# Two-bank PSUM copies, an earlier output 1, and weight-gradient units held for the end, in the backward pass of a grouped-query decode block

## The chip, the cores and the metric

The kernel runs on one core of one Trainium2 chip. The metric is the device time of one execution in microseconds (us), the median of several executions. The kernel before takes 1144.1 us (median of 4 runs, 1141.7 to 1148.9; the first three had a median of 1144.4).

The trace names the engines PE (TensorE matmul), PEld (its weight loads), DVE (VectorE), ACT (ScalarE), POOL (GpSimd, which issues the stores) and SP (SyncE, which issues the loads). Line numbers such as L1162 are lines of the kernel that was run, so the same statement has another number in each kernel; the text says which is which.

## The reference

Two layers, each an attention over a long key/value cache followed by an MLP, and then the gradients of everything with respect to a given output gradient. The sizes that matter: batch 2, one query position, 32 query heads over 4 key/value heads, 16384 cached positions, head size 128, model width 1024, MLP width 3584.

```python
x = A_x
x = x + A(layernorm(x), k_cache, v_cache, wq, wo)     # attention
x = x + B(layernorm(x), w1, b1, w2, b2)               # layernorm, gelu MLP
x = x + A(layernorm(x), ...);  x = x + B(layernorm(x), ...)
out, vjp = jax.vjp(f, A_x, k_cache, v_cache, wq, wo, w1, b1, w2, b2)
return out, *vjp(grad_out)    # out_0; dx = out_1; dK = out_2; dV = out_3; dwq = out_4; dwo, dw1, db1, dw2, db2
```

The outputs dK and dV are as large as the caches: 64 tiles of 1 MB, computed and stored in the last third of the kernel, together with about 32 MB of weight gradients. The caches are read several times in bf16. All of it passes through one core's DMA: 449 MB.

## The kernel before

The change touches the last third: the loop that works off chunks of the caches. In each step of that loop TensorE transposes V tiles, computes scores, and makes "pairs" (half a tile of dK or dV each) and "dW units" (512 columns of a weight gradient). Pairs and dW units are matmuls into PSUM, followed by copies that turn fp32 in PSUM into bf16 in SBUF. The Trainium skill ("PSUM — Partial Sum Buffer", Terms) says that PSUM has 8 banks of 2 KiB per partition and that one matmul's output fits in one bank, which is 512 fp32 columns; the matmuls of this loop agree, the widest writes 512 columns. Four banks go round for this work and for a few small products between (`X`); the other four serve transposes (2), an accumulator and small things.

```python
X = [px([128, 512], F32, "xm%d" % i) for i in range(4)]      # four tiles of one bank, in rotation
def mx(): return nxt("x", X)

def kv_pair(w, i, h):                                        # half a dK or dV tile
    ...
    pss = [mx() for _ in range(4)]
    for b in range(2):
        for r in range(4):
            PE.matmul(pss[r][:, b * 256:(b + 1) * 256], lhsT=blk[32 * r:32 * r + 32, ...], rhs=Qm[32 * r:32 * r + 32, ...], ...)
    for r in range(4):
        evac_cast(sv_[:, 2 * h:2 * h + 2, r], pss[r][:]..., 512)      # to ScalarE or VectorE, the less loaded
    if h == 1: store(...)                                    # 1 MB, issued by GpSimd

def dw_units(...):  # for each 512 columns:
        ps = mx()
        PE.matmul(ps[:], lhsT=xrows[p:p + 4, ...], rhs=yrows[p:p + 4, ...], ...)   # 4 rows
        evac_cast(sv_[:, j, c0:c0 + 512], ps[:], 512)
        # after the last of a tile: store(...)

def load_tile(): return (by_store or by_read).popleft()      # a tile whose store was issued, else one that was read

while 2 * m < NS + 12 or late or fill or late_pe or m <= max(v_at) + 2:
    ...                                                      # transposes, scores, pairs of this step
    step_fill(1 if m < NCH else 5)                           # 5 dW units of 512 columns
    pump(NLD + 3 if m < NCH else NLD, 3)                     # loads, at most 7 open
    m += 1
g0 = attn_in_bwd(0, g1, dn0)                                 # last layer-norm backward, after everything
col_to_row_f32(g0, DJ, out_1..., "o1")                       # output 1
```

A matmul into a bank waits until the copy out of it is done. The traces show matmuls starting in program order, so that what comes later in TensorE's queue waits too (an example with 1.04 us stands below, with the profile after).

## Time and profile before

| | before |
|---|---|
| median time | 1144.1 us |
| bytes moved | 449.3 MB, 394 GB/s over the span |
| middle, 840 to 1100 us | 422 GB/s, DMA full |
| opening of the last third, 730 to 840 us | 347 GB/s |
| from the last dqT (1115.95 us) to the end | 24.8 us at 220 GB/s |

The first lines are from the page of the kernel before: its span, TensorE's busy time, and the clock granted to TensorE (tenths) and the DMA rate in 40 equal slices of 28.5 us.

```profile
span 1140.8 us, 39972 instructions
PE 954.6 (84%) x17567; PEld 736.6 (65%) x17567; DVE 633.4 (56%) x1347; ACT 566.2 (50%) x1418; POOL 64.7 (6%) x117
...
PEclk9989785597999876999998899989779868896785
...
GB/s 371 424 424 424 425 423 413 408 379 354 423 424 424 425 302 424 410 377 407 373 423 419 349 354 355 314 331 309 400 423 422 421 420 422 423 422 421 424 419 247
```

Nine slices of the last third are at 420 GB/s or above and one at 419; the last slice is at 247. Windows give the same by stage. The columns: stretch, its length, then for each engine its busy us in the stretch and the number of instructions; then the granted clock, the DMA engines' mean busy share, and GB/s. The last two stretches are cut at the last dqT, the query gradient that the end of the kernel depends on.

```profile
840.00:900.00 60.00, 52.90 (x690) 32.89 (x687) 48.41 (x85) 46.09 (x89) 9.51 (x16) 0.86 1.02 422
900.00:1000.00 100.00, 91.55 (x1122) 55.10 (x1120) 77.11 (x135) 71.85 (x139) 16.33 (x28) 0.79 1.02 422
1000.00:1100.00 100.00, 90.25 (x1230) 56.22 (x1228) 76.76 (x135) 71.01 (x137) 14.25 (x24) 0.81 1.02 422
1100.00:1116.00 16.00, 11.69 (x129) 5.39 (x125) 11.67 (x20) 10.90 (x21) 2.14 (x4) 0.66 1.00 420
1116.00:1140.80 24.80, 14.57 (x114) 6.44 (x114) 10.63 (x26) 7.90 (x14) 3.15 (x5) 0.50 0.54 220
```

DMA is full until 1116 us. And beside it TensorE is busy 90 to 92 us of every 100, VectorE 77, ScalarE 71: the compute engines keep up with DMA, but not by much.

The stores of the tail, in order of time on GpSimd (start, duration, and in brackets how long GpSimd had been idle and for what):

```profile
1124.41 0.53 POOL L1126 DMA_DIRECT2D out_dram<-keepV  x1 [12.02 <-DVE keepV L166]
1126.29 0.53 POOL L1126 DMA_DIRECT2D out_dram<-keepK  x1 [1.35 <-ACT big L163]
1128.13 0.77 POOL L1126 DMA_DIRECT2D out_dram<-big  x1 [1.31 <-ACT big L163]
1131.17 0.77 POOL L1126 DMA_DIRECT2D out_dram<-big  x1 [2.27 <-ACT big L163]
1136.65 0.55 POOL L202 DMA_DIRECT2D out_dram<-o_row  x1 [4.71 <-DVE o_row L201]
```

No store is issued for 12 us, and output 1 is the last.

### The profile page before, as it was taken

The page shows a single profiled execution, that of the slowest core. Times are in us where ns is not written, and L with a number is a line of the kernel's source. Part 1 is how long each engine was busy: PE and PEld are TensorE (multiplying, and loading weights), DVE is VectorE, ACT ScalarE, POOL GpSimd, SP SyncE. Part 2 cuts the span into 40 slices and gives each one's busy share as a digit, 9 for nine tenths or more (in the row PEclk, how much of TensorE's full clock was granted, in tenths as well). Part 3 has the DMA queues.
Part 4 walks back from the last instruction along what each step waited for, and adds up shares of the span by engine and source line. Part 5 has one row for each costly group of instructions (what it writes and reads, how often), then busy time and mean ns, then how long its engine had stood idle before and what let it go on. Part 6 is the DMA issues. An engine that isn't in the chain of part 4 may idle for free. (4 is left out here: it accounts for less than half of the span.)

```text
span 1140.8 us, 39972 instructions
## 1 busy us (share of the span) xinstructions
PE 954.6 (84%) x17567; PEld 736.6 (65%) x17567; DVE 633.4 (56%) x1347; ACT 566.2 (50%) x1418; POOL 64.7 (6%) x117
## 2 busy tenths in 40 slices
PE   4988896487879885899987789988898989999885
PEld 3867674387767765888776688765555555555552
DVE  1535442133545433544845355768678868786784
ACT  0534351022535330344554444668677767776673
POOL 0000000000000000000000000001111112111111
PEclk9989785597999876999998899989779868896785
DMA  9999999998999989999999999887999999999996
GB/s 371 424 424 424 425 423 413 408 379 354 423 424 424 425 302 424 410 377 407 373 423 419 349 354 355 314 331 309 400 423 422 421 420 422 423 422 421 424 419 247
DMA packets 89130, 449.30 MB, mean 394 GB/s; under 512 B 7026, under 2 KB 7026, under 8 KB 49788
## 3 DMA queue, kind: packets, MB, share of 16 engines
q1 hardware_dynamic: 72204, 348.17, 75.4%
q0 software_dynamic: 16752, 98.59, 20.8%
q8 instruction: 137, 2.24, 0.7%
q14 instruction: 37, 0.30, 0.1%
HBM read 348.14 MB, written 98.58 MB: 392 GB/s over the span
## 5 line engine op out<-in xcount | busy, mean ns | idle before, releaser
L155 ACT COPY kT<-tp 128x512 int32<-128x512 int32 x209 | 122.8, 587 | 252.0 <-PE tp L421 243.3
L158 DVE COPY kT<-tp 128x1024 bf16<-128x1024 bf16 x159 | 108.6, 691 | 109.2 <-PE tp L421 97.3
L421 PE MATMUL tp<-ident,kv_K 128*128 128x128 bf16 x1728 | 144.5, 233 | 4.5 <-DMA kv_K<-in_A_k_cache_dram 4.4
L421 PEld LDWEIGHTS <-kv_K 128*128 128x128 bf16 x1728 | 109.6, 104 | 5.3 <-DMA kv_K<-in_A_k_cache_dram 5.2
L166 DVE CAST big<-xm 128x512 bf16<-128x512 f32 x135 | 88.1, 686 | 25.3 <-PE xm L1162 11.7
L163 ACT CAST big<-xm 128x512 bf16<-128x512 f32 x162 | 88.3, 594 | 24.6 <-PE xm L1162 12.7
L574 PEld LDWEIGHTS <-kT 128*128 128x128 bf16 x2048 | 76.6, 98 | 27.8 <-issue 21.4
L574 PE MATMUL sc<-qT_bf,kT 128*128 128x8 bf16 x2048 | 92.0, 171 | 0.3 <-issue 0.3
L538 ACT ACTIVATE e_all<-sc,negm 128x64 bf16<-128x64 f32 x256 | 77.1, 345 | 1.1 <-DVE negm L533 1.0
L307 PEld LDWEIGHTS <-wt 128*128 128x128 bf16 x1696 | 49.2, 104 | 43.7 <-issue 14.8
L421 PE MATMUL tp<-ident,kv_V 128*128 128x128 bf16 x864 | 70.1, 227 | 8.5 <-DMA kv_V<-in_A_v_cache_dram 7.6
L271 PE MATMUL wtp<-ident,wt 128*128 128x128 bf16 x928 | 73.9, 225 | 3.7 <-issue 2.5
L166 DVE CAST keepK<-xm 128x512 bf16<-128x512 f32 x91 | 59.1, 686 | 21.7 <-PE xm L1244 17.7
L453 PE MATMUL acc_all<-kv_V,e_all 128*16 128x256 bf16 x864 | 46.5, 296 | 26.4 <-DMA kv_V<-in_A_v_cache_dram 13.7
L163 ACT CAST keepK<-xm 128x512 bf16<-128x512 f32 x105 | 56.8, 594 | 23.8 <-PE xm L1244 23.1
L158 DVE COPY wT<-wtp 128x1024 bf16<-128x1024 bf16 (+1 forms) x64 | 40.7, 641 | 46.6 <-PE wtp L271 43.5
L155 ACT COPY wT<-wtp 128x512 int32<-128x512 int32 (+1 forms) x60 | 34.3, 572 | 61.7 <-PE wtp L271 47.5
L421 PEld LDWEIGHTS <-kv_V 128*128 128x128 bf16 x864 | 55.4, 102 | 10.7 <-DMA kv_V<-in_A_v_cache_dram 8.3
L166 DVE CAST keepV<-xm 128x512 bf16<-128x512 f32 (+1 forms) x80 | 52.5, 686 | 16.3 <-PE xm L1244 12.8
L163 ACT CAST keepV<-xm 128x512 bf16<-128x512 f32 (+1 forms) x93 | 50.3, 593 | 20.1 <-PE xm L1244 18.2
L538 ACT ACTIVATION_READ_ACCUMULATOR e_all<-sc,negm 128x1 f32 x256 | 60.1, 235 | 0.0
L271 PEld LDWEIGHTS <-wt 128*128 128x128 bf16 x928 | 56.3, 100 | 4.4 <-issue 3.0
(350 smaller groups left out, 1786.9 us busy)
## 6 DMA issues: line engine op xcount, KB each, us to landing
kv_K<-in_A_k_cache_dram SPq DMA_DIRECT2D x81, 1024.0 KB, 12.3
kv_V<-in_A_v_cache_dram SPq DMA_DIRECT2D x81, 1024.0 KB, 12.1
out_dram<-big POOLq DMA_DIRECT2D x36, 1024.0 KB, 18.5
wt<-in_A_wo_dram SPq DMA_DIRECT2D x32, 1024.0 KB, 10.2
wt<-in_B_w_dram SPq DMA_DIRECT2D x32, 896.0 KB, 14.2
out_dram<-keepK POOLq DMA_DIRECT2D x21, 1024.0 KB, 18.3
out_dram<-keepV POOLq DMA_DIRECT2D x19, 1024.0 KB, 15.0
wt<-in_A_wq_dram SPq DMA_DIRECT2D x16, 1024.0 KB, 9.0
```

The source lines that it names most:

```text
L155: S.copy(out=dst.bitcast(I32), in_=src.bitcast(I32))
L158: V.tensor_copy(out=dst, in_=src)
L163: S.copy(out=dst, in_=src)
L166: V.tensor_copy(out=dst, in_=src)
L271: PE.transpose(tp[:, o, :], wv[:, j, (o0 + o) * 128:(o0 + o + 1) * 128], ident[:])
L307: PE.matmul(fps[:, jo, :].rearrange("p (a b) -> p a b", b=2), lhsT=wv[:, j, jo * 128:(jo + 1) * 128], rhs=xT_bf[:, j0 + j, :].unsqueeze(1) ...
L421: PE.transpose(tp[:, j, :], cv[:, b * 8 + j, :], ident[:])
L453: PE.matmul(self.acc[cg:cg + 16, :], lhsT=coef(u), rhs=self.cv[:, t:t + 2, :].rearrange("p t d -> p (t d)"), start=False, stop=True, tile_ ...
L538: S.activation(out=e_all[:, g, f * half:(f + 1) * half, l, h, :], in_=sc[g][f][:, h, :].rearrange("p (a b) -> p a b", b=2), func=ACT.Exp, ...
L574: PE.matmul(sc[g][f][:, :, t % TH], lhsT=kT[:, j, :], rhs=q_bf[:, g, :], start=True, stop=True)
```

## The change

Its intent: fewer, larger copies out of PSUM; an opening that prefetches more; stores left over for the end so that DMA has work while the last query gradient is finished; and output 1 not at the very end.

```diff
 # 1. two-bank copies (in pairs and in dW units)
-    X = [px([128, 512], F32, "xm%d" % i) for i in range(4)]
+    XX = [ps_xx.tile([128, 2, 512], F32, name="xx%d" % i, tag="xx") for i in range(2)]
+    X = [XX[i // 2][:, i % 2, :] for i in range(4)]            # single banks are halves of these
-        for r in range(4):
-            evac_cast(sv_[:, 2 * h:2 * h + 2, r], pss[r][:]..., 512)
+        for r in range(2):
+            evac_cast(sv_[:, 2 * h:2 * h + 2, 2 * r:2 * r + 2]..., pss[r][:]..., 1024)
-                for c0 in range(0, ny, 512): ...                # dW: one matmul, one copy of 512
+                for c0 in range(0, ny, 1024): ...               # dW: two matmuls, one copy of 1024
 # 2. opening
-        return (by_store or by_read).popleft()
+        return (by_read or by_store if opening["on"] else by_store or by_read).popleft()
-    pump(NLD + 3, 4)
+    pump(NLD + 3, 3)
     ... two weight loads two chunks later; score banks swapped; two zero copies gone
 # 3. dW units held for the last ten steps, fewer loads open there
-        step_fill(1 if m < NCH else 5)
-        pump(NLD + 3 if m < NCH else NLD, 3)
+        step_fill(1 if m < NCH else 3 if m >= MF else 2 + bool(late), 0 if m >= MF else 20)
+        pump(NLD + 3 if m < NCH else NLD if m < MF + 4 else NLD - 1, 3)
 # 4. last dq to output 1 at once (and the last chunk's accumulation one step earlier)
+            tail.extend(in_rows(quarters[kv], kv))              # products, layer-norm backward, output 1
-    g0 = attn_in_bwd(0, g1, dn0)                                # was after the loop
-    col_to_row_f32(g0, DJ, out_1..., "o1")
 # 5. last dWq over 128 partitions, padded with zeros, stored in three pieces
     ... (cut: columns padded so that the transposes for dW rows write 32 rows)
+            late.extend(dw_units(nz, qz, None, [(0, 4), (4, 2), (6, 2)], 0, D, ...))
```

The bytes that move stay the same.

## The prediction

> **What bounds the kernel now.** The 16 DMA engines: the slice rows show them 98 to 102 % busy at 421 to 424 GB/s in most of the span, and 449.3 MB at 424 GB/s would take 1060 us (an estimate) of the 1140.8. The Trainium skill ("DMA: Bandwidth & Descriptors", Measured) gives 425 GB/s for a large transfer; the trace agrees. Only stretches in which DMA starves can pay. By the windows, 800 to 1116 us runs at 410 to 423 GB/s: nothing to win. Before 700 us the change touches almost nothing. Two stretches are left:
>
> - The tail. In 4 us windows from 1116 us: 256, 35, 272, 398, 388, 13 GB/s. Those 24.8 us move about 5.5 MB, 13 us of work at 424: some 12 us are lost. The chain that ended last shows why: last dqT at 1115.95, dq transposed and copied until 1118.1, dWq matmuls and pairs until 1131.2, no store issued from 1111.9 to 1124.4; then the last layer-norm backward (1130.5 to 1132.8), fp32 transposes and a 0.68 us cast twice, and the output-1 store at 1136.65.
> - The opening, 730 to 790 us: 306, 229, 367, 351, 243, 279 GB/s in 10 us windows, about 18 us lost. The SP queue's waits there are loads held by the landing of an older store from their tile (52 us in 4 waits), while ScalarE and VectorE are 76 to 96 % busy from 750 to 790.
>
> **What the change does.**
> 1. Two-bank copies: two 128x512 copies take 1.29 us on VectorE and 1.07 on ScalarE; one of 1024 about 1.22 and 1.05 (an estimate from 0.686 and 0.594 single). 0 to 2 us, all in the opening. Back-to-back pairs now wait for a whole two-bank copy, so their 1.8 us period does not shrink.
> 2. Opening: loads go first to tiles freed by compute, one more tile may be taken, two weight loads come two chunks later, two 0.6 us zero copies vanish. I give this 5 us of the 18; the copy engines limit the rest.
> 3. dW held: the instruction order shows 4 MB more dW stores among the last ones. The last loads run ahead of them, so the last dq comes earlier and stores are queued while dq is finished. This fills most of the hole around 1120.
> 4. Output 1 at once: its chain runs between the last pairs; the 5 us between the last big store's issue and output 1's leave the end.
> 5. Zero-padded dWq: the tail's clock is 0.50 although PE is 70 to 88 % busy with 4-row operands; 128 rows may raise it, 16 matmuls from 0.43 to about 0.22 us, hardly 1 us in effect since copies then bind.
>
> Tail: 12 us lost become about 4 (output 1 ended 4 us after its issue), so 8. Sum: 8 + 5: 1144.4 - 13 = **1131 us**, range 1122 to 1141. Chances: faster by over 2 % 0.09, within 2 % 0.90, slower 0.01.
>
> **What would show it.** Bytes stay 449 MB. Right: windows of the last 25 us near 400 GB/s without the 35 GB/s hole, the last dqT several us earlier, output 1's store no longer last by 5 us; shorter waits of loads on store landings in 730 to 790; the middle still at 421 to 424. Step 5: clock above 0.5 at the end.
>
> **What would make it wrong.** The held dW copies load ScalarE and VectorE (already 88 to 92 % busy at 1093 to 1103), the last steps become copy-bound and dq does not come earlier; the opening keeps its gap or moves it later because tiles are merely taken sooner; the coarser PSUM hand-over starves the copies; or the opening recovers all 18 us, over 2 %.

## More of the kernel before

How TensorE and the copies hand PSUM over shows in the waits of the middle, 840 to 1100 us (columns: who waited for whom, us in all, times, longest). L1162 is the dW matmul, L166 and L163 are the copies on VectorE and ScalarE.

```profile
PE xm L1162 <- ACT big L163: 2.5, 7, 0.5
...
PE xm L1162 <- DVE big L166: 2.1, 7, 0.6
```

All such waits of the dW matmul add up to 8 us there.

## The result, and the profile after

The changed kernel is correct and takes 1195.3 us (median of 4 runs, 1192.9 to 1197.1). Ratios in this document are the mean time of one kernel's runs over that of the kernel before in the same rounds, so they are not quite the ratio of the medians quoted. Here the ratio is 1.044, with a 95% interval of 1.040 to 1.048: slower by 4.4%, where 1131 us had been forecast, and slower given a chance of 1%.

The same lines of the page after (slices of 29.8 us):

```profile
span 1193.1 us, 39480 instructions
PE 974.3 (82%) x17567; PEld 749.6 (63%) x17567; DVE 622.2 (52%) x1174; ACT 559.6 (47%) x1225; POOL 68.1 (6%) x120
...
PEclk9988895588989957999988999977778677676675
...
GB/s 374 424 424 425 424 425 412 406 304 423 424 425 424 413 338 415 369 395 373 422 419 344 372 347 350 329 350 377 371 369 397 394 369 406 350 362 349 345 214 212
```

The copies did become cheaper: VectorE and ScalarE are busy 11 and 7 us less, in 366 fewer instructions. But from slice 30 on the DMA rate stays below 400 in every slice but one, where it was 419 or more until the last. The windows of the kernel after, cut at its last dqT (1165.3 us):

```profile
840.00:900.00 60.00, 50.93 (x617) 31.37 (x614) 40.69 (x47) 39.04 (x51) 7.64 (x13) 0.74 0.98 390
900.00:1000.00 100.00, 82.81 (x1034) 50.71 (x1033) 65.91 (x78) 62.61 (x81) 13.43 (x23) 0.76 0.99 392
1000.00:1100.00 100.00, 85.33 (x961) 51.23 (x959) 61.44 (x73) 59.30 (x74) 15.99 (x24) 0.69 0.92 356
1100.00:1165.30 65.30, 53.79 (x588) 32.56 (x584) 40.81 (x47) 38.77 (x47) 8.13 (x14) 0.71 0.70 287
1165.30:1193.10 27.80, 15.88 (x130) 6.57 (x130) 12.34 (x23) 9.01 (x9) 4.14 (x7) 0.56 0.51 209
```

Call "lost" the length of a stretch times (1 - rate / 424), the time in which DMA could have moved what it did not. Before: 1.2 us lost from 840 to 1100, 0.2 from there to the last dqT, 11.9 in the tail. After: 28.4, 21.1 and 14.1. The difference is 50.3 us, and the spans differ by 52.3. So nearly the whole loss is in the middle and its continuation, in the stretch of which the prediction had said "nothing to win", and where there was much to lose. All engines do less per microsecond there, TensorE too. Nobody is busier: somebody waits. The page says the same in its chain of work that ended last (by engine, as shares of the span): before, the compute engines have about 2% of the span in it; after, a third.

```profile
PE 2%; issue 1%; DVE 0%; ACT 0%; POOL 0%; POOLq 0%; DVEq 0%
```

```profile
PE 23%; ACT 6%; DVE 4%; issue 1%; POOLq 0%; POOL 0%; DVEq 0%; ACTq 0%
```

The waits name it. In the kernel after L1185 is the dW matmul, L165 and L162 are the copies:

```profile
PE xx L1185 <- DVE big L165: 6.4, 6, 1.3
PE xx L1185 <- ACT big L162: 6.0, 10, 0.8
PE xx L1185 <- ACT keepV L162: 4.0, 7, 1.1
```

All waits of the dW matmul for copies add up to 22.8 us from 840 to 1100 us, against 8 before, although fewer units pass; the longest is 1.3 us, against 0.6. The small products that use the same tiles (L1033, L468) wait 11.1 us, against 7.4. The waits name the place; that they make up all of the 28.4 us lost there is not shown. One such place in order of time (x8 is a group of eight; the duration is of the group; weight loads are left out):

```profile
1005.42 1.23 DVE L165 CAST big<-xx 128x1024 bf16<-128x1024 f32 x1 [1.02 <-PE xx L1268]
1005.52 1.02 ACT L162 CAST big<-xx 128x1024 bf16<-128x1024 f32 x1
1006.70 1.02 PE L1185 MATMUL xx<-rowsA,rowsB 4*128 4x512 bf16 x4 [1.04 <-DVE big L165]
1007.33 1.23 DVE L165 CAST big<-xx 128x1024 bf16<-128x1024 f32 x1 [0.68 <-PE xx L1185]
1007.65 0.87 PE L1464 MATMUL tpm<-ident,keepV 128*128 128x128 bf16 x8
1007.76 1.01 ACT L162 CAST big<-xx 128x1024 bf16<-128x1024 f32 x1 [1.22 <-PE xx L1185]
```

Both tiles are shut, each by one long copy. TensorE stands for 1.04 us, and so do all the transposes (L1464) behind it in its queue; then VectorE stands for 0.68 us and ScalarE for 1.22 us waiting for TensorE. They take turns instead of working side by side. The stores are not held by DMA any more: the median time from a 1 MB store's issue to its landing fell from 18.5 to 9.0 us for the largest group, which fits a DMA queue with less in it.

```profile
out_dram<-big POOLq DMA_DIRECT2D x36, 1024.0 KB, 18.5
```

```profile
out_dram<-big POOLq DMA_DIRECT2D x30, 1024.0 KB, 9.0
```

### The profile page after: what moved, and what is told of

The parts are those of the page before. It is cut to its first block, busy times and chain, and to the rows that moved or that the text cites. A ratio compares the mean times of both kernels' runs of the same rounds, so it can differ in the third digit from the quotient of the medians.

```text
span 1193.1 us, 39480 instructions
## 1 busy us (share of the span) xinstructions
PE 974.3 (82%) x17567; PEld 749.6 (63%) x17567; DVE 622.2 (52%) x1174; ACT 559.6 (47%) x1225; POOL 68.1 (6%) x120
## 3 DMA queue, kind: packets, MB, share of 16 engines
q0 software_dynamic: 16768, 98.59, 20.1%
## 5 line engine op out<-in xcount | busy, mean ns | idle before, releaser
L421 PE MATMUL tp<-ident,kv_K 128*128 128x128 bf16 x1728 | 141.9, 230 | 4.3 <-DMA kv_K<-in_A_k_cache_dram 4.2
L165 DVE CAST big<-xx 128x1024 bf16<-128x1024 f32 (+1 forms) x67 | 80.3, 1199 | 43.8 <-PE xx L1185 25.7
L574 PEld LDWEIGHTS <-kT 128*128 128x128 bf16 x2048 | 75.8, 98 | 26.8 <-issue 21.1
L162 ACT CAST big<-xx 128x1024 bf16<-128x1024 f32 x67 | 66.9, 1000 | 43.0 <-PE xx L1268 22.0
L271 PE MATMUL wtp<-ident,wt 128*128 128x128 bf16 x928 | 78.1, 233 | 2.6 <-issue 1.2
L307 PEld LDWEIGHTS <-wt 128*128 128x128 bf16 x1696 | 48.8, 103 | 44.2 <-issue 15.4
L162 ACT CAST keepV<-xx 128x1024 bf16<-128x1024 f32 (+1 forms) x59 | 59.0, 1006 | 34.8 <-PE xx L1268 22.5
L165 DVE CAST keepK<-xx 128x1024 bf16<-128x1024 f32 (+1 forms) x48 | 57.1, 1189 | 24.0 <-PE xx L1185 10.0
L453 PE MATMUL acc_all<-kv_V,e_all 128*16 128x256 bf16 x864 | 45.4, 289 | 28.4 <-DMA kv_V<-in_A_v_cache_dram 15.0
L165 DVE CAST keepV<-xx 128x1024 bf16<-128x1024 f32 (+1 forms) x45 | 54.0, 1199 | 26.2 <-PE xx L1268 17.2
L162 ACT CAST keepK<-xx 128x1024 bf16<-128x1024 f32 (+2 forms) x51 | 49.0, 962 | 35.1 <-PE xx L1185 17.4
L271 PEld LDWEIGHTS <-wt 128*128 128x128 bf16 x928 | 59.7, 104 | 3.3 <-issue 2.0
L1328 PE MATMUL dp<-wdo,kT 128*128 128x64 bf16 x896 | 60.9, 223 | 0.0
```

What stands on the lines that cost most here:

```text
L162: S.copy(out=dst, in_=src)
L165: V.tensor_copy(out=dst, in_=src)
L271: PE.transpose(tp[:, o, :], wv[:, j, (o0 + o) * 128:(o0 + o + 1) * 128], ident[:])
L421: PE.transpose(tp[:, j, :], cv[:, b * 8 + j, :], ident[:])
L453: PE.matmul(self.acc[cg:cg + 16, :], lhsT=coef(u), rhs=self.cv[:, t:t + 2, :].rearrange("p t d -> p (t d)"), start=False, stop=True, tile_ ...
L574: PE.matmul(sc[g][f][:, :, t % TH], lhsT=kT[:, j, :], rhs=q_bf[:, g, :], start=True, stop=True)
```

## The experiments

The first question is whether the two-bank copies cost the time (theory A), or the schedule: the held dW units, the fewer loads, the new order of tiles (theory B). Each diff is against the kernel named.

### e1_one_bank: the kernel after, on single banks again

```diff
-    XX = [ps_xx.tile([128, 2, 512], ...) for i in range(2)]
+    X = [px([128, 512], F32, "xm%d" % i) for i in range(4)]
-            evac_cast(..., pss[r][:]..., 1024)         # two copies of 1024 in a pair, one in a dW unit
+            evac_cast(..., pss[r][:]..., 512)          # four of 512, two of 512
```

> The kernel after with every 1024-column copy made of two 512-column copies out of single banks again (four separate one-bank tiles; units, order, held dW, opening and tail stay as in the kernel after). Theory A (the coarser hand-over of PSUM, two pairs in place of four banks, stalls TensorE): the time falls from 1195 us to 1125 to 1145, and the windows from 840 to 1100 us are back at 415 to 424 GB/s. Theory B (held dW, fewer loads, new tile order): stays at 1180 or more.

Measured: 1144.0 us (1138.6 to 1147.1), 0.997 of before (0.9935 to 1.0009). The two-bank copies, with the two-bank tiles that they need, account for the whole loss. The middle:

```profile
840.00:900.00 60.00, 55.73 (x736) 33.86 (x732) 49.59 (x86) 46.50 (x90) 8.67 (x15) 0.86 1.01 423
900.00:1000.00 100.00, 83.62 (x1087) 50.81 (x1087) 72.03 (x129) 66.51 (x128) 14.46 (x25) 0.82 1.01 422
1000.00:1100.00 100.00, 93.31 (x1057) 56.24 (x1055) 74.00 (x129) 67.73 (x130) 17.29 (x25) 0.72 1.01 413
```

DMA is full again, and the dW matmul's waits for copies are 6.0 us in all from 840 to 1100 us (8 before, 22.8 after). The other parts of the change together are worth 0.3%, with an interval that includes nothing, where 13 us (1.1%) had been forecast.

### e2_before_two_bank: the kernel before, with the two-bank copies alone

The edit is part 1 of the change on the kernel before, and dW units of 1024 columns drained 2 or 3 per step.

> The kernel before with only the two-bank copies (pairs and dW), the bank moves they need, and dW units of 1024 columns drained 2 or 3 per step in place of 5 of 512. Theory A: 1175 to 1200 us, with the middle windows at 350 to 390 GB/s. Theory B: 1138 to 1150 us.

Measured: 1197.9 us, 1.045 (1.042 to 1.048); 376, 392 and 374 GB/s in the three windows of the middle, and 25.9 us of such waits of the dW matmul. Theory A again, from the other side.

### e3_kv_one, e4_dw_one: two-bank copies in one of the two places

The kernel after, with single-bank copies only in pairs (e3) or only in dW units (e4). The single banks are then halves of the two-bank tiles, as in the kernel after.

> The kernel after with single-bank copies only in the dK/dV pairs; dW keeps the two-bank copies. Theory A: part of the 50 us comes back; a pair uses all four banks either way, so if dW units are what blocks TensorE most of the loss stays (1170 to 1190), if the pairs are, most of it goes (1140 to 1155). Theory B: no change, 1190 to 1200.

> The kernel after with single-bank copies only in dW; the dK/dV pairs keep the two-bank copies. Theory A: the complement of the run with single-bank pairs, together they give back about the 50 us (if the parts add). Theory B: no change, 1190 to 1200.

Measured: e3 1253.0 us (1.093), e4 1289.6 us (1.126). Both are slower than the kernel after, which neither theory had expected: less of the cause made it worse. Either single banks are bad beside double ones, or the half of a tile is not a bank of its own.

### e8_halves: single banks, cut as halves of two-bank tiles

```diff
-    X = [px([128, 512], F32, "xm%d" % i) for i in range(4)]          # e1
+    XX = [ps_xx.tile([128, 2, 512], ...) for i in range(2)]
+    X = [XX[i // 2][:, i % 2, :] for i in range(4)]
```

> The one-bank version, only with its four single banks cut as halves of two two-bank tiles; every matmul and copy is the same. Theory T (a tile is handed over as a whole: a matmul into one half waits for the copy of the other half, which is why both mixed versions were slower than the kernel after): 1250 us or more. If the hand-over goes by bank: 1144 us, as with four separate tiles.

Measured: 1319.1 us (2 runs, 1.154), against 1144.0 with the same matmuls and the same copies on four tiles. The program's framework places the waits, and it hands a tile over as a whole: a matmul into one half waits for the copy out of the other. So this kernel has two units to hand over, not four, and each is handed over for every 512 columns; the next run shows that copies out of the two halves wait for each other as well. In e3 and e4 one of the two places works in this way, which fits their being slower than the kernel after.

### e9_split: the kernel after, its two-bank tiles copied by two engines

```diff
-            evac_cast(..., pss[r][:]..., 1024)
+            evac_cast(..., pss[r // 2][:, r % 2]..., 512)    # for r in range(4); dW the same way
```

> The kernel after, with each two-bank tile still filled and handed over as a whole, but copied by two 512-column copies, in most cases one on ScalarE and one on VectorE at the same time, in place of one of 1024. Theory W (what costs is that a pair of banks stays shut for one long copy of 1.0 to 1.2 us, against 0.6 to 0.7): 1150 to 1180 us. Rival (what costs is the pairing itself: two hand-over units in place of four, and single-bank users that shut a pair): 1185 us or more.

Measured: 1271.4 us, 1.112. Theory W had foreseen a gain. The trace says why the experiment did not test what it should have: the two copies of one tile run one after the other.

```profile
1006.74 0.69 DVE L165 CAST keepV<-xx 128x512 bf16<-128x512 f32 x1
...
1007.47 0.59 ACT L162 CAST keepV<-xx 128x512 bf16<-128x512 f32 x1 [1.02 <-DVE keepV L165]
...
1008.10 0.59 PE L1185 MATMUL xx<-rowsA,rowsB 4*128 4x512 bf16 x2 [0.81 <-ACT keepV L162]
```

ScalarE waits for VectorE's copy from the other bank of the same tile, though both only read it, and TensorE waits for both: the tile is shut for 0.69 + 0.59 us and a hand-over, longer than for one copy of 1.2 us. That both copies write to one SBUF tile is not the reason: in e1, where the banks are tiles of their own, copies into one SBUF tile run side by side.

```profile
901.87 1.07 ACT L162 CAST keepxV<-xm 128x512 bf16<-128x512 f32 x2 [0.41 <-PE xm L1260]
901.90 1.29 DVE L165 CAST keepxV<-xm 128x512 bf16<-128x512 f32 x2 [0.98 <-PE xm L1260]
```

So the run is no test of copy length.

### e13_two_single and e14_by_row: two units with short copies, and four

To separate the count of units from the length of the copy and from shared tiles, the pair was rewritten so that it needs one bank at a time; then the rotation was cut to two tiles.

```diff
 # e14, on e1_one_bank
-        pss = [mx() for _ in range(4)]
-        for b in range(2):
-            for r in range(4): PE.matmul(pss[r]...)
-        for r in range(4): evac_cast(..., pss[r][:]..., 512)
+        for r in range(4):
+            ps = mx()
+            for b in range(2): PE.matmul(ps[:, b * 256:(b + 1) * 256], ...)
+            evac_cast(sv_[:, 2 * h:2 * h + 2, r], ps[:]..., 512)
 # e13, on e14
-    X = [px([128, 512], F32, "xm%d" % i) for i in range(4)]
+    X = [px([128, 512], F32, "xm%d" % i) for i in range(2)]
```

> The one-bank version (1144 us) with only two single banks in rotation in place of four, and each dK/dV pair worked off row block by row block (two matmuls into a bank, then its copy of 512 columns). If the number of hand-over units is what counts, it is as slow as the kernel after or slower: 1185 to 1240 us, though every copy is short and no tile is shared. If the long copy or the shared tile is what counts: 1140 to 1160.

> Control for the run with two single banks: the one-bank version with four banks, and the pairs worked off row block by row block. Expected 1138 to 1150 us, as the one-bank version, since only the order of eight matmuls and four copies in a pair changes.

Measured: 1439.2 us with two banks (1.258), 1139.3 us with four (0.994, 0.991 to 0.998). Every copy is short and no tile is shared in either, so neither is needed for a loss: too few units under way are enough. But two single banks also hold only half the columns of the kernel after, and the loss is far beyond the 1185 to 1240 us expected; so the run does not say how much of the kernel after's loss is the count alone. The middle of the run with two, 900 to 1000 us:

```profile
900.00:1000.00 100.00, 81.68 (x617) 40.21 (x615) 45.91 (x73) 43.18 (x76) 8.19 (x14) 0.52 0.68 247
```

247 GB/s, and a granted clock of 0.52. The kernels on one picture: four units of 512 columns, 1139 to 1151 us (all such runs, those below included); two of 1024, 1188 to 1198; two tiles handed over, in one place or both, for each 512, 1253 to 1319; two of 512, 1439. With the same columns in all, two units in place of four cost some 50 us; with two units, half the columns cost some 250 us more. So both count: into how many units the columns are divided, and how many columns may be under way. At equal columns, half as many units are also units that stay shut twice as long for a copy (1.22 us against 0.69 on VectorE), and small products shut a double tile; no run separates these.

### e17_after_row: the kernel after, pairs tile by tile

The pair's matmuls reordered so that the four of the first tile come first, then its copy of 1024, then the second tile.

> The kernel after, two-bank tiles and copies kept, with each pair worked off tile by tile (four matmuls into a tile, then its copy of 1024 columns), so that the first copy starts two matmuls earlier. If the count of hand-over units is what counts, this takes back little: 1180 to 1196 us. If the late start of the first copy was the cause: 1150 or less.

Measured: 1187.7 us, 1.036 (1.032 to 1.040): about 8 us better than the kernel after, no repair.

### e5, e6, e7, e15: the other parts of the change, one at a time

e5_no_hold is e1 with `step_fill(1 if m < NCH else 2 + m % 2, 0)` and `pump(NLD + 3 if m < NCH else NLD, 3)`: opening and tail, without the hold. e7_tail_only is e5 with part 2 of the diff undone. e6_opening_only is the kernel before with part 2, and e15_hold_only the kernel before with part 3 (40 units of 512 columns kept; 6 per step at the end).

> The one-bank version of the kernel after (which took 1144 us), and in it the hold taken away: dW units are drained 2 or 3 per step from the start (as many 512-column pieces as before), none kept back, and 7 loads stay allowed open to the end. Theory H (the hold makes the last steps bound by the copy engines and brings the last dq late: 1120.2 us there against 1115.95 before): 1132 to 1140 us, last dqT before 1115. Rival: the hold does nothing or helps, and the opening's and the tail's gains were never there: 1143 or more.

> The kernel before with the opening's part alone (loads to tiles freed by compute first, one tile more, weight loads two chunks later, score banks swapped, no zero copies). From the windows of the one-bank version, which moved 1.7 MB more between 740 and 780 us: 1139 to 1142 us. If the gap is only moved later: 1144 to 1148.

> The kernel before with the tail's part alone (last dq to output 1 at once, last quads one step earlier, zero-padded last dWq; units of 1024 columns from single banks; no hold, old opening). As predicted for steps 4 and 5: 1137 to 1141 us. If the end is set by dWq's copies and stores whatever output 1 does: 1143 to 1147.

> The kernel before with the hold alone (40 units of 512 columns kept for the last ten steps, 6 per step there, 4 or 6 before, one load fewer open at the end). If the hold works as predicted: last dqT before 1113 us and the time 1135 to 1141. If it makes the last steps bound by compute: last dqT after 1118 and 1146 to 1153.

| run | parts | median us | ratio to before (95%) |
|---|---|---|---|
| e6_opening_only | opening | 1141.9 | 0.998 (0.996 to 1.001) |
| e7_tail_only | output 1 early, padded dWq | 1149.5 | 1.005 (1.003 to 1.008) |
| e15_hold_only | hold | 1146.9 | 1.001 (0.998 to 1.004) |
| e5_no_hold | opening, tail | 1146.2 | 1.002 (0.9995 to 1.005) |
| e1_one_bank | opening, hold, tail | 1144.0 | 0.997 (0.9935 to 1.001) |

The expectation for e5 (1132 to 1140 us) failed: taking the hold away did not bring the gain out. The opening is worth about 2 us, which its interval does not tell from nothing; the hold alone nothing; the tail is half a per cent in the wrong direction, outside both ranges expected for e7 (it also brings the dW units of 1024 columns and the padded columns, which were not tried alone).

### e10, e11, e12: can the tail be made shorter?

e10_open_hold is e1 with the old tail; e11_early_out is e10, only that the layer-norm backward and output 1 follow the last products at once, and the last dWq (4-row matmuls, as before) is stored in three pieces; e12_open_out is e6 with that same early output.

> Opening and hold of the kernel after on single banks, with the old tail (last dWq from four rows, last quads at their old step, layer-norm backward and output 1 after everything). If the parts add (opening -0.2 to -0.3 %, hold -0.5 % by the runs so far, tail +0.5 %): 1133 to 1139 us, 0.99 of the kernel before. If hold only helped because the new tail hurt: 1141 or more.

> The run with opening, hold and old tail, only that the layer-norm backward and output 1 follow the last products at once, before most of the last dWq, which is stored in three pieces. The old tail took 24.8 us from the last dqT to the end, with output 1's store issued 20.7 us after dqT; here output 1 should be out 14 to 16 us after dqT, and the end 20 to 22 us after it: 2 to 4 us less than with the old tail. If the last dWq's copies are pushed back by as much as output 1 is pulled forward: no gain, 24 to 27 us.

> The kernel before (units of 512 columns, single banks, no hold) with the opening's part, output 1 right after the last products, and the last dWq stored in three pieces. The best parts so far: opening alone took 0.998 of before, the early output 1 took 0.3 % off the version with the hold. If they add: 1135 to 1140 us, 0.994 to 0.997 of before, with the stretch from the last dqT to the end at 22 to 24.5 us against 24.4 to 24.8. If TensorE's in-order queue at half clock makes the tail a fixed sum (what output 1 gains, the last dWq loses): 0.998 again.

Measured: e10 1150.6 us (1.007, 1.004 to 1.010), e11 1147.1 us (1.004, 1.001 to 1.006), e12 1142.1 us (0.998, 0.997 to 0.9998). The parts do not add: e10 was expected at 0.99. (It keeps the dW units of 1024 columns and the padded columns too.) The tails of the profiled runs, one run each:

| run | last dqT, us | output 1's store after dqT | end after dqT | GB/s from dqT to end |
|---|---|---|---|---|
| before | 1115.95 | 20.7 | 24.8 | 220 |
| e1_one_bank | 1120.2 | 20.1 | 25.1 | 240 |
| e7_tail_only | 1124.1 | 20.8 | 26.9 | 233 |
| e15_hold_only | 1124.0 | 20.9 | 25.0 | 178 |
| e11_early_out | 1120.4 | 16.4 | 24.3 | 179 |
| e12_open_out | 1113.1 | 16.4 | 26.3 | 224 |
| e14_by_row | 1108.5 | 20.3 | 29.3 | 254 |
| e16_open_row (below) | 1109.7 | 19.8 | 27.2 | 240 |
| after | 1165.3 | 23.5 | 27.8 | 209 |

No version brought the end closer to dqT than 24.3 us. Where output 1 did come out earlier after dqT (e11, e12), the rest came later. The stores at the end of e12:

```profile
1127.39 0.53 POOL L1127 DMA_DIRECT2D out_dram<-keepxV  x1 [2.39 <-issue]
1129.51 0.53 POOL L201 DMA_DIRECT2D out_dram<-o  x1 [1.58 <-DVE o L200]
1130.75 0.75 POOL L1127 DMA_DIRECT2D out_dram<-big  x1 [0.72 <-ACT keepV L161]
1132.15 0.73 POOL L1127 DMA_DIRECT2D out_dram<-keepV  x1 [0.65 <-ACT keepV L161]
```

Output 1 is issued 16.4 us after dqT (20.7 before), but the last dWq store 19.1 us after it (15.2 before). What is put forward pushes back what stood there: the clock is 0.50 here, and the 16 dWq matmuls start 0.43 us apart when they follow each other. But TensorE is busy only 14.8 of these 26.3 us (before, 14.6 of 24.8), so its queue alone does not fix the length of the tail; what does is not shown.

### e16 and e18: does the order of the pair help by itself?

e18_before_row is the kernel before with only the pair of e14; e16_open_row adds the opening.

> The kernel before with the opening's part and the pairs worked off row block by row block on four single banks. If these two are what made 1139 us: 1134 to 1140 us, 0.991 to 0.996 of before. If the hold and the tail are needed too: 1141 to 1144.

> The kernel before with nothing but the pairs worked off row block by row block. Expected 1139 to 1145 us, 0.996 to 1.000: the middle is bound by DMA, so the earlier copies can only pay in the opening (18 us lost there) and in the tail.

Measured: e18 1144.2 us (0.998, 0.996 to 1.001), e16 1140.7 us (0.997, 0.994 to 0.999). The lowest median is e14_by_row, 1139.3 us, which keeps opening, hold and tail of the change on four single banks. It beats both kernels, by 0.6% and by 4.7% of the medians. Its interval overlaps those of e16 and e1, so which of its parts are needed beside the order of the pair is not settled.

## Why the prediction was wrong, point by point

**Step 1, the two-bank copies: here it failed.** The prediction said: "0 to 2 us, all in the opening. Back-to-back pairs now wait for a whole two-bank copy, so their 1.8 us period does not shrink." The durations were right (1.22 us on VectorE, 1.01 on ScalarE for 1024 columns; 1.22 and 1.05 were estimated). The conclusion was not: removing the two-bank copies took 1195.3 us to 1144.0, putting them alone on the kernel before gave 1197.9. The estimate counted the engine time saved and compared the pair's period, in which all four banks are used either way. It did not count how many units may be under way. With dW units between the pairs, four independent banks let TensorE fill one while two are copied and one waits; with two tiles, both are soon shut, and all that follows in TensorE's queue waits with them. The prediction named this as a risk ("the coarser PSUM hand-over starves the copies") and gave slower a chance of 1%.

**"Nothing to win" in the middle: true, and misread.** A stretch bound by DMA cannot gain from compute, but it can lose. TensorE's 90 to 92 us of 100 and the ScalarE and VectorE shares beside it were on the page. The check that was missing: how much may the compute side slow down before DMA starves? The DMA share alone does not answer it. A second loss came on top: the granted clock in the three windows of the middle fell from 0.86, 0.79, 0.81 to 0.74, 0.76, 0.69. The Trainium skill ("TensorE: Matmul & The Clock Gate", A second HAM failure mode: psum-queue depth-cycling) describes a kernel whose TensorE idles briefly between groups of matmuls while it cycles PSUM banks, and whose clock is throttled again and again. The windows agree in direction: the kernels in which TensorE waits more for copies have a lower clock (0.59 to 0.69 in e8, 0.52 to 0.61 in e13). How much of the 50 us is the clock's was not separated; a low clock alone is not enough, for in e1 it was 0.72 from 1000 to 1100 us and DMA still moved 413 GB/s.

**Step 2, the opening:** predicted 5 us, measured 0.2% (about 2 us, with an interval of 5 us gained to 1 lost). In the profiles 730 to 840 us rose from 347 to 356 GB/s, by the formula above 20.0 us lost became 17.6. The direction fits; the size is half or less, and not clear of noise.

**Step 3, the hold:** predicted that "the last dq comes earlier". With the hold alone it came later, 1124.0 us against 1115.95, and in e1 at 1120.2, with 312 GB/s from 1100 us to it. Nor did held stores fill the hole: from dqT to the end the hold alone moved 178 GB/s, against 220 before. Of the failures listed in the prediction this looks like the first (the last steps have to do the held copies as well), but that is argued: these are single profiles, and of the 8 us in e15 some 4 were lost before 730 us, ahead of the hold (402 and 338 GB/s in 0 to 640 and 640 to 730 us, against 404 and 344). In e14 dqT did come early, at 1108.5 us with DMA at 422 GB/s from 1100 us until then; but it came at 1109.7 in e16, which has no hold, so this is the work of the opening and the order of the pair. On the kernel before, the hold is worth nothing (1.001).

**Step 4, output 1 at once:** predicted that "the 5 us between the last big store's issue and output 1's leave the end". In e1 output 1's store was still the last and came 20.1 us after dqT, against 20.7; the end came 25.1 us after it, against 24.8. When it was really put forward (e11, e12), the dWq stores moved back by nearly as much. The step that failed is the reading of the tail as a chain with a free end: no order that was tried made the stretch from dqT to the end shorter than 24.3 us (24.8 before). What holds it at that length stays open.

**Step 5, the padded dWq:** predicted "128 rows may raise" the clock, "hardly 1 us in effect". In e1 it was 0.56 from 1120 to 1130 us and 0.78 from 1130 to 1140, where the kernel before had 0.50 in both. The other profiles bear the direction out: from the last dqT to the end the clock was 0.50 in every kernel with the last dWq from 4 rows (nine runs, e11 and e12 with the early output 1 among them), and 0.56 to 0.64 in the padded ones on four single banks (e1, e5, e7, e14) and in the kernel after. In four padded kernels that were much slower (e3, e4, e8, e13) it was 0.50 again, so padding alone is not enough. No time came of it.

So of the 13 us forecast for steps 2 to 5 the runs found between 1 lost and 7 gained (e1: 0.3%, give or take 0.4%), and of the 0 to 2 us of step 1 a loss of some 50.

## What to carry to other kernels

Count the PSUM hand-over units before widening a copy: half as many units of twice the size save a little engine time per copy (18 us of VectorE and ScalarE together here), and may cost more in overlap between TensorE and the engines that empty PSUM (some 50 us here). In this framework a tile was a unit of hand-over as a whole, so halves of one tile were not two buffers, not even for two readers (e8, e9). And in a stretch that is bound by DMA, look at how busy the next engine is: here TensorE was busy 90 to 92 us of 100 beside a full DMA, and a change that made it wait showed in the time.

## What the Trainium skill lacked or had wrong

- "PSUM — Partial Sum Buffer" gives the banks and what a matmul's output may fill, and "Perfetto Trace Analysis" (Matmuls) advises rotating independent matmuls through different banks; I found nothing on how many units must be in flight, or on what fewer and larger ones cost. Here: four single banks 1139 to 1151 us, two tiles of two banks 1188 to 1198 us, two single banks 1439 us.
- No page that I read says that the waits placed by the program's framework can treat a tile of several banks as one, readers included. Here: the same matmuls and copies on halves of two tiles 1319 us, on four tiles 1144 us; in e9_split ScalarE's copy waited 1.02 us for VectorE's from the other bank.
- "TensorE: Matmul & The Clock Gate": the page ties the clock to how busy TensorE has been; I found no word on what operands of few rows do to it. In the tail of the kernel before the clock stayed at 0.50 while TensorE was busy 8.85 of 10 us (1120 to 1130 us), some 7 us of it in matmuls of 4 or 32 rows; with a last dWq of 128 rows on four single banks the tail had 0.56 to 0.64 (four profiles; not isolated).
